# Two load queues, a pause in the zero fills, and three stage buffers in an attention and FFN backward kernel

## The chip, the cores and the metric

The kernel runs on one core of a Trainium2 chip. The metric is the device time of one execution in microseconds (us), the median of several runs. A profile gives the span of one execution, which is about 1.7 us below the time of that run (886.2 against 887.95 us before); positions in time below are read from the profiles, in us from the start of the span.

## The reference

It is one decode step (one query row) of an attention block and a gated FFN, with all gradients (shortened here):

```python
W = min(4096, max(256, Sk // 4))        # 4096 of the 32768 cached rows are attended
k = jnp.repeat(k_cache[:, :, Sk - W:, :], rep, axis=1)      # 8 groups, 2 heads each
v = jnp.repeat(v_cache[:, :, Sk - W:, :], rep, axis=1)
scores = jnp.einsum("bhqd,bhkd->bhqk", q, k) * (Dh ** -0.5)
o = jnp.einsum("bhqk,bhkd->bhqd", _softmax(scores, axis=-1), v)
# ...
h  = x + _A_ref(_layernorm(x), k_cache, v_cache, wq, wo)    # one query row, D = 448
h2 = h + _B_ref(_layernorm(h), w_gate, w_up, w_down)        # (g * u) @ w_down, F = 1792
# ...
_out, _vjp = jax.vjp(_f, x, k_cache, v_cache, wq, wo, w_gate, w_up, w_down)
return (_out, *_vjp(grad_out))          # the output and eight gradients
```

For time, one fact matters. The gradients of the two caches have 8 x 32768 x 256 elements each, but only the last 4096 rows of a group are attended. The other 28672 rows of each group must be written as zeros: 112 zero fills of 2 MB, 234.9 MB of the 332.75 MB that the kernel moves.

## The kernel before

The zero fills come from one zeroed tile in the core's memory (SBUF), 16 KB in each of 128 partitions. All but nine are sent by GpSimd, the nine others by SyncE, which also does every load and every other store:

```python
    LD = nc.sync
    ZQ = nc.gpsimd
    # ...
    late_jobs = [(out_2, G - 1, 5, 7, ZW), (out_3, G - 1, 0, 7, ZW)]
    for g in range(G):
        for o in (out_2, out_3):
            if g == G - 1 and o is out_3:
                continue
            reg = zero_rows(o, g, 0, 5 if g == G - 1 else NZ, ZW)
            for i in range(reg.shape[0]):
                ZQ.dma_start(out=reg[i], in_=zeros)
    # ... at the end of the program:
        for o, g, n0, n1, f in late_jobs:
            reg = zero_rows(o, g, n0, n1, f)
            for i in range(reg.shape[0]):
                LD.dma_start(out=reg[i], in_=zeros)
```

The work has three parts. *Attention* goes over eight groups; K and V of a group (2 MB each) are loaded into buffers that earlier groups free. The *FFN* goes over four blocks of weights in one buffer, so the loads of a block wait until the block before is computed; its gate and up rows are 1 KB long:

```python
    def load_ffn(f0, nw):
        n = 128 * nw
        LD.dma_start(out=wd_b[:, 0:nw, :], in_=B_w_down[f0:f0 + n, :].rearrange("(p w) n -> p w n", w=nw))
        for i, w in enumerate((B_w_gate, B_w_up)):
            LD.dma_start(out=w_b[i][:, 0:3 * n].rearrange("p (c f) -> p c f", c=3), in_=w[0:384, f0:f0 + n].rearrange("(p c) f -> p c f", c=3))
            LD.dma_start(out=wB_b[i][:, 0:n], in_=w[384:D, f0:f0 + n])
```

The *backward loop* follows, once more over the eight groups. Each group computes its gradients of V and K into two stage buffers of 2 MB and stores them; weight gradients are stored in between:

```python
    stage = [seq(MB), seq(MB + 16 * KB), seq(S[6])]
    # ...
            stV, stK = stage[stc % 2], stage[(stc + 1) % 2]
            if it >= 6:
                stV, stK = stage[(stc - 12) % 3], stage[(stc - 11) % 3]
            stc += 2
            # ... matmuls into PSUM, copied into stV and stK by VectorE and ScalarE
            for o_ap, st_ in ((out_3, stV), (out_2, stK)):
                LD.dma_start(out=o_ap[0, g, Sk - W:, :].rearrange("(p t) d -> p t d", t=T), in_=st_)
```

A scheduler orders the instructions of each engine; the program order is only a start. It moved the nine late fills of SyncE forward, among the K loads of attention.

Of the kernel before, what the change touches and what calls it, by code (L numbers as in the profile page):

```python
# [13 lines left out]
D = 448  # L14
H = 16
G = 8
Dh = 256
W = 4096
T = 32
# [4 lines left out]
Sk = 32768  # L24
EPS = 1e-5
SCALE = 1.0 / 16.0
ZW = 8192
NZ = (Sk - W) * Dh // (128 * ZW)
KB = 512


@with_exitstack
def kernel(
        ctx, tc, A_x, A_k_cache, A_v_cache, A_wq, A_wo, B_x, B_w_gate, B_w_up, B_w_down, grad_out,
           out_0, out_1, out_2, out_3, out_4, out_5, out_6, out_7, out_8):
    nc = tc.nc
    LD = nc.sync
    ZQ = nc.gpsimd

    const = ctx.enter_context(tc.tile_pool(name="const", bufs=1))  # L40
# [5 lines left out]

    MB = 128 * KB
    RB = 152 * KB
    TOTAL = 196 * KB
    arena = const.tile([128, TOTAL], bf16)  # L50

    def ar(off, n):
        return arena[:, off:off + n]

    def seq(off):
        return ar(off, T * Dh).rearrange("p (t d) -> p t d", d=Dh)

    zeros = ar(0, ZW)
    S = [16 * KB * (i + 1) for i in range(7)]
    V_at = [seq(o) for o in (S[5], S[0], S[1], S[2], S[3], S[4], S[6], S[5])]  # L60
    K_at = [seq(o) for o in (RB, S[6], S[4], S[5], RB, S[6], S[5], RB)]
    wqA = ar(S[2], 24 * KB).rearrange("p (c j) -> p c j", c=3)
    wqB = ar(S[2] + 24 * KB, 4 * KB)
    M_off = [MB + 4 * KB * g for g in range(6)] + [RB + 28 * KB, RB + 32 * KB]
# [6 lines left out]
    wo_sb = ar(RB, 28 * KB).rearrange("p (j n) -> p j n", n=D)  # L71
    wd_b = ar(RB + 28 * KB, 4 * D).rearrange("p (w n) -> p w n", n=D)
    w_b = [ar(RB + 63 * KB // 2 + 3 * KB * i, 3 * KB) for i in range(2)]
    wB_b = [ar(RB + 75 * KB // 2 + KB * i, KB)[0:64] for i in range(2)]
# [6 lines left out]
    ok_rows = ar(RB + 83 * KB // 2, 2 * KB)[0:H].bitcast(f32).rearrange("p (k d) -> p k d", k=2)  # L81
    h_row = ar(RB + 42 * KB, 2 * D)[0:1].bitcast(f32)

    stage = [seq(MB), seq(MB + 16 * KB), seq(S[6])]
    dq_bc = ar(RB + 8 * KB, H * Dh)
    Rbig = [ar(o, 8 * KB).rearrange("p (l n) -> p l n", l=8) for o in (RB + 16 * KB, S[1] + 24 * KB)]
    VT_slot = [ar(RB + (24 + 2 * i) * KB, 2 * KB).rearrange("p (e t k) -> p e t k", t=4, e=2) for i in range(3)]
# [10 lines left out]
    x_bf = const.tile([1, D], bf16)  # L98
    LD.dma_start(out=x_bf[:], in_=A_x.rearrange("a b d -> (a b) d"))
    dh2_bc = const.tile([128, D], bf16)  # L100
    LD.dma_start(out=dh2_bc[:], in_=grad_out.rearrange("a b d -> (a b) d").to_broadcast([128, D]))
    wq_A = A_wq[0:384, :].rearrange("(p c) j -> p c j", c=3)
    wq_B = A_wq[384:D, :].rearrange("r (h j) -> (r h) j", h=2)
    LD.dma_start(out=wqA, in_=wq_A)
    LD.dma_start(out=wqB, in_=wq_B)

    ident_bf = const.tile([128, 128], bf16)
    make_identity(nc, ident_bf[:])
# [11 lines left out]
    def zero_rows(o, g, n0, n1, f):  # L120
        reg = o[0, g, 0:Sk - W, :].rearrange("s d -> (s d)")[n0 * 128 * ZW:n1 * 128 * ZW]
        return reg.rearrange("(n p f) -> n p f", p=128, f=f)

    late_jobs = [(out_2, G - 1, 5, 7, ZW), (out_3, G - 1, 0, 7, ZW)]
    for g in range(G):
        for o in (out_2, out_3):
            if g == G - 1 and o is out_3:
                continue
            reg = zero_rows(o, g, 0, 5 if g == G - 1 else NZ, ZW)
            for i in range(reg.shape[0]):  # L130
                ZQ.dma_start(out=reg[i], in_=zeros)  # L131


    pair_f = const.tile([128, 64], f32)
# [68 lines left out]
        nc.vector.scalar_tensor_tensor(out=r[:], in0=t[:], scalar=rstd, in1=plus, op0=ALU.mult, op1=ALU.add)  # L203
        return r

    def load_kv(dst, cache, g):
        LD.dma_start(out=dst, in_=cache[0, g, Sk - W:, :].rearrange("(p t) d -> p t d", t=T))

    for g in range(3):
        load_kv(K_at[g], A_k_cache, g)  # L210
        load_kv(V_at[g], A_v_cache, g)

    rstd1, xnT_f, X1_b = layernorm(x_bf[:], bf16, "ln1")
    d2_ps = ps_t.tile([128, 4], f32, tag="tmp")
# [11 lines left out]
    qT_bf = const.tile([128, 32], bf16)  # L226
    nc.vector.tensor_copy(out=qT_bf[:], in_=qT_ps[:])

    load_kv(V_at[3], A_v_cache, 3)
    load_kv(V_at[4], A_v_cache, 4)  # L230

    def load_wo(j0, j1):
        LD.dma_start(out=wo_sb[:, j0:j1, :], in_=A_wo.rearrange("(p j) n -> p j n", j=32)[:, j0:j1, :])

    def load_ffn(f0, nw):
        n = 128 * nw
        LD.dma_start(out=wd_b[:, 0:nw, :], in_=B_w_down[f0:f0 + n, :].rearrange("(p w) n -> p w n", w=nw))
        for i, w in enumerate((B_w_gate, B_w_up)):
            LD.dma_start(out=w_b[i][:, 0:3 * n].rearrange("p (c f) -> p c f", c=3), in_=w[0:384, f0:f0 + n].rearrange("(p c) f -> p c f", c=3))
            LD.dma_start(out=wB_b[i][:, 0:n], in_=w[384:D, f0:f0 + n])  # L240

    pT_all = const.tile([128, G, T, 2], bf16)
    oT_f = const.tile([128, 2, H], f32)
# [32 lines left out]
    with tc.tile_pool(name="ps_x", bufs=1, space=bass.MemoryType.PSUM) as ps_x, \  # L276
# [69 lines left out]
        for g in range(G):  # L346
            p_f = p_next
            if g + 1 < G:
                p_next = scores(g + 1)
            moments(g, p_f)  # L350
            if g == 0:
                load_kv(K_at[3], A_k_cache, 3)
                load_kv(K_at[4], A_k_cache, 4)
            elif g == 1:
                load_kv(K_at[5], A_k_cache, 5)
            elif g == 2:
                load_kv(V_at[5], A_v_cache, 5)
            elif g == 3:
                load_kv(K_at[6], A_k_cache, 6)
                load_wo(19, 27)  # L360
            elif g == 4:
                load_kv(K_at[7], A_k_cache, 7)
            elif g == 5:
                load_kv(V_at[6], A_v_cache, 6)
            elif g == 6:
                load_kv(V_at[7], A_v_cache, 7)
                load_wo(27, 32)
        load_wo(0, 19)
        load_ffn(*FB[0])
        nc.vector.tensor_copy(out=ok_rows, in_=ok_ps[:])  # L370

    with tc.tile_pool(name="ps_mid", bufs=2, space=bass.MemoryType.PSUM) as ps_mid, \
# [27 lines left out]
        for q, (f0, nw) in enumerate(FB):  # L400
            n, cb = 128 * nw, f0 // 128
            if q:
                load_ffn(f0, nw)
            dh_f = workm.tile([128, 4], f32, tag="dh_f")
            for w in range(nw):
                nc.vector.tensor_tensor_reduce(out=dg_b[:, 0:D], in0=wd_b[:, w, :], in1=dh2_bc[:], scale=1.0, scalar=0.0,
                                               op0=ALU.mult, op1=ALU.add, accum_out=dh_f[:, w:w + 1])
            gu_ps = ps_mid.tile([128, 2, 4], f32, tag="mid")
            for i in range(2):
                wv = w_b[i][:, 0:3 * n].rearrange("p (c f) -> p c f", c=3)  # L410
                for w in range(nw):
                    for k in range(3):
                        nc.tensor.matmul(gu_ps[:, i, w:w + 1], lhsT=wv[:, k, w::nw], rhs=X2_b[:, k:k + 1], start=(k == 0), stop=False)  # L413
                    nc.tensor.matmul(gu_ps[:, i, w:w + 1], lhsT=wB_b[i][:, w:n:nw], rhs=X2_b[0:64, 5:6], start=False, stop=True)  # L414
            gu_f = workm.tile([128, 2, 4], f32, tag="gu_f")
            nc.vector.tensor_copy(out=gu_f[:, :, 0:nw], in_=gu_ps[:, :, 0:nw])  # L416
            for i in range(2):
                nc.vector.tensor_tensor(out=dgu_f[:, i, cb:cb + nw], in0=dh_f[:, 0:nw], in1=gu_f[:, 1 - i, 0:nw], op=ALU.mult)
            nc.vector.tensor_tensor(out=hh_f[:, cb:cb + nw], in0=gu_f[:, 0, 0:nw], in1=gu_f[:, 1, 0:nw], op=ALU.mult)
            nc.vector.tensor_copy(out=hh_bf[:, cb:cb + nw], in_=hh_f[:, cb:cb + nw])  # L420
            for i in range(2):
                spread(dg_b[:, i * KB:i * KB + n], diag_b, dgu_f[:, i, cb:cb + nw], nw, ps_mid, "mid")
            for w in range(nw):
                nc.tensor.matmul(ffn_ps[:], lhsT=hh_bf[:, cb + w:cb + w + 1], rhs=wd_b[:, w, :], start=(cb + w == 0), stop=(cb + w == NF - 1))
            for i in range(2):
                dg = dg_b[:, i * KB:i * KB + n]
                wv = w_b[i][:, 0:3 * n].rearrange("p (c f) -> p c f", c=3)
                for c in range(3):
                    nc.vector.tensor_tensor_reduce(out=wv[:, c, :], in0=wv[:, c, :], in1=dg, scale=1.0, scalar=0.0,
                                                   op0=ALU.mult, op1=ALU.add, accum_out=dhn2[:, c, 2 * q + i:2 * q + i + 1])  # L430
                nc.vector.tensor_tensor_reduce(out=wB_b[i][:, 0:n], in0=wB_b[i][:, 0:n], in1=dg[0:64, :], scale=1.0, scalar=0.0,
                                               op0=ALU.mult, op1=ALU.add, accum_out=dhnB[:, 2 * q + i:2 * q + i + 1])

        def close(dn, dcat):

# [58 lines left out]
    with tc.tile_pool(name="work2", bufs=2) as work2, tc.tile_pool(name="lnw", bufs=1) as lnw, \  # L494
# [82 lines left out]

        order = [1, 2, 3, 4, 5, 6, 7, 0]
        V_now = V_at[:]
        V_now[0] = seq(S[0])  # L580
        stc = 0
        for it, g in enumerate(order):
            V_sb = V_now[g]
# [5 lines left out]
                else:  # L589
                    nc.vector.tensor_copy(out=XT, in_=ps)  # L590
            dpT_ps = dots(V_sb, VT_slot, vpad[it % 2], rows2, ps_t, "tmp", evac)
            if it == 0:
                load_kv(V_now[0], A_v_cache, 0)
            if it == 4:
                LD.dma_start(out=wq2A, in_=wq_A)
# [20 lines left out]
            RB_ = Rbig[it % 2] if it >= 3 else Rbig[0]  # L616
            for l in range(8):
                nc.vector.tensor_scalar(out=RB_[:, l, :], in0=R_sb[:], scalar1=tl_f[:, l:l + 1], scalar2=None, op0=ALU.mult)
            stV, stK = stage[stc % 2], stage[(stc + 1) % 2]
            if it >= 6:  # L620
                stV, stK = stage[(stc - 12) % 3], stage[(stc - 11) % 3]
            stc += 2
            for l in range(8):
                for qp in range(2):
# [5 lines left out]
                    t = 4 * l + 2 * qp  # L630
# [27 lines left out]
                nc.vector.tensor_copy(out=dx_bf[:, 384:D], in_=dx_ps[0:1, 384:D])  # L658
                LD.dma_start(out=out_1.rearrange("a b d -> (a b) d"), in_=dx_bf[:])

        for o, g, n0, n1, f in late_jobs:
            reg = zero_rows(o, g, n0, n1, f)
            for i in range(reg.shape[0]):
                LD.dma_start(out=reg[i], in_=zeros)

# [1 line left out]
_INS = ['A_x', 'A_k_cache', 'A_v_cache', 'A_wq', 'A_wo', 'B_x', 'B_w_gate', 'B_w_up', 'B_w_down', 'grad_out']  # L667
# [26 lines left out]
```

## Time and profile before

| | before |
|---|---|
| median of 4 runs, on the chip that also ran the change | 887.32 us |
| bytes moved | 332.75 MB |
| attention ends (last output matmul of a group) | 365.0 us |
| output weights have landed | 410.8 us |
| backward loop starts (first query-gradient matmul) | 607.4 us |
| last copy into a stage buffer | 874.5 us |
| span | 886.2 us |

The profile cuts the span into 40 equal slices. A digit is the busy share of a slice in tenths; the last row is what the DMA engines moved. These are its rows for TensorE and DMA:

```profile
PE   0669999996059675504202020127986476644121
...
DMA  8999999999999999999999999999999198354444
GB/s 339 430 431 429 429 430 426 433 427 427 419 430 429 416 424 429 425 428 427 428 427 428 428 428 429 428 427 425 422 417 387 56 412 324 132 238 189 189 190 190
```

DMA is full (about 429 GB/s) up to the 31st slice, some 670 us, and then runs at 208 GB/s on average (680 to 875 us). TensorE, on the other hand, has long holes where DMA is full: the core waits for its own loads while the fills go through. The queues of the same page (packets, MB, and the time of their packets as a share of 16 engines) show who moves what; q0 is GpSimd's queue, q1 SyncE's:

```profile
q0 software_dynamic: 14832, 216.01, 57.5%
q1 hardware_dynamic: 13750, 116.19, 31.6%
...
HBM read 51.59 MB, written 280.59 MB: 375 GB/s over the span
```

The chain of waits follows the work that ended last backwards; each line is a start, a length and what was waited for. For a DMA the length runs from its issue to its landing. The engine that needs it may have worked for a part of that time, so a piece can be much longer than the engine's own wait. The longest DMA pieces after the start:

```profile
213.92 38.56 another core or an unknown queue
...
285.69 15.63 DMA arena<-in_A_v_cache_dram
...
326.34 16.25 DMA arena<-in_A_v_cache_dram
...
365.05 45.70 DMA arena<-in_A_wo_dram
...
434.35 40.05 DMA arena<-in_B_w_up_dram
...
485.24 39.58 DMA arena<-in_B_w_up_dram
...
534.79 37.56 DMA arena<-in_B_w_up_dram
...
668.90 28.69 DMA out_dram<-arena
...
803.71 10.57 DMA out_dram<-arena
...
828.96 10.57 DMA out_dram<-arena
```

The piece at 213.92 is a wait for K. Its load sits in SyncE's queue behind the nine fills that the scheduler had moved forward. Then come V loads of two groups, the output weights, and 37 to 40 us for each of three FFN blocks. In the backward loop a store of weight gradients takes 28.69 us. The two pieces of 10.57 us are stage stores that a stage copy waits for.

Why an FFN load of 1.3 MB takes 40 us is shown by the packets of the two queues from 375 to 395 us, when the first block is loaded:

```profile
q0 software_dynamic: 554, 8.04, 93.9%
q1 hardware_dynamic: 553, 0.53, 7.6%
```

The two queues take turns, one packet each: 554 against 553. But a packet of a fill has 16 KB and one of the load 1 KB or less, so the load gets 0.53 of 8.58 MB, 27 GB/s.

### The profile page before, as it was taken

The numbers are of one execution on the slowest core, as the hardware profiler recorded it, in microseconds if no ns is written. First come the engines' busy times: TensorE is split into PE (matmuls) and PEld (weight loads), VectorE is DVE, ScalarE is ACT, GpSimd is POOL, SyncE is SP. The second block draws the span as 40 slices with busy tenths as digits, with TensorE's granted clock in tenths as the row PEclk, the third lists the DMA queues.
The fourth block names the chain that finished last, engine by engine and source line by source line (L and its number), as shares of the span: only waits on it lengthen the run. The fifth ranks groups of instructions, "written<-read, shape, count | busy, mean of one in ns | idle before, by whom it ended". The sixth has DMA issues, their size and how long they took to land.

```text
span 886.2 us, 8621 instructions
## 1 busy us (share of the span) xinstructions
PE 458.8 (52%) x3193; PEld 248.1 (28%) x3193; DVE 370.8 (42%) x1243; ACT 198.7 (22%) x325; POOL 59.7 (7%) x112
## 2 busy tenths in 40 slices
PE   0669999996059675504202020127986476644121
PEld 0435455453025242302100000016643233221000
DVE  2036535633015244200403111083396779986453
ACT  0341331330031300000000000001462443433342
POOL 4000000000001000000000010010000000000000
PEclk9969999999579897856555555556997687666555
DMA  8999999999999999999999999999999198354444
GB/s 339 430 431 429 429 430 426 433 427 427 419 430 429 416 424 429 425 428 427 428 427 428 428 428 429 428 427 425 422 417 387 56 412 324 132 238 189 189 190 190
DMA packets 28624, 332.75 MB, mean 375 GB/s; under 512 B 2979, under 2 KB 7206, under 8 KB 8742
## 3 DMA queue, kind: packets, MB, share of 16 engines
q0 software_dynamic: 14832, 216.01, 57.5%
q1 hardware_dynamic: 13750, 116.19, 31.6%
q8 instruction: 25, 0.41, 0.2%
q14 instruction: 17, 0.14, 0.0%
HBM read 51.59 MB, written 280.59 MB: 375 GB/s over the span
## 4 chain that ended last, share of the span: by engine, by line
PE 38%; DMA 34%; DVE 16%; another core or an unknown queue 4%; ACT 4%; issue 1%; SPq 1%; DVEq 0%; ACTq 0%
DMA arena<-in_B_w_up_dram 13%; PE M_ps L327 12%; PE ok_ps L331 6%; DMA out_dram<-arena 6%; PE rows_ps L267 6%; DMA arena<-in_A_k_cache_dram 5%; DMA arena<-in_A_wo_dram 5%; PE tr_ps L264 4%; DMA arena<-in_A_v_cache_dram 4%; DVE arena L636 3%; DVE arena L635 3%; PE d_ps L628 2%; DVE arena L458 2%; ACT arena L282 2%; PE dqb_ps L501 2%
## 5 line engine op out<-in xcount | busy, mean ns | idle before, releaser
L323 DVE TENSOR_SCALAR arena<-arena,p_f 128x256 bf16<-128x256 bf16 x512 | 109.4, 281 | 132.0 <-PE M_ps L327 132.0
L327 PE MATMUL M_ps<-arena 128*128 128x512 bf16 x512 | 124.9, 387 | 22.3 <-DMA arena<-in_A_v_cache_dram 22.3
L264 PE MATMUL tr_ps<-ident_bf,arena 128*128 128x128 bf16 x1024 | 88.2, 237 | 75.2 <-DMA arena<-in_A_k_cache_dram 49.7
L264 PEld LDWEIGHTS <-arena 128*128 128x128 bf16 x1024 | 67.3, 106 | 119.6 <-DMA arena<-in_A_k_cache_dram 50.2
L267 PE MATMUL rows_ps<-arena,vpad 128*16 128x512 bf16 x256 | 84.4, 429 | 31.0 <-DVE arena L590 15.0
L282 ACT COPY arena<-tr_ps 128x1024 bf16<-128x1024 bf16 x64 | 61.8, 1015 | 145.3 <-PE tr_ps L264 145.3
L131 POOL DMA_DIRECT2D out_dram<-arena x103 | 55.1, 536 | 576.6 <-DMA out_dram<-arena 576.6
L628 PE MATMUL d_ps<-arena,rT 32*128 32x512 bf16 x256 | 39.9, 518 | 71.9 <-DVE arena L636 46.1
L327 PEld LDWEIGHTS <-arena 128*128 128x128 bf16 x512 | 47.0, 100 | 75.6 <-DMA arena<-in_A_v_cache_dram 22.7
L413 PE MATMUL gu_ps<-X_b,arena 128*128 128x1 bf16 x84 | 7.2, 177 | 111.5 <-DMA arena<-in_B_w_gate_dram 70.4
L331 PE MATMUL ok_ps<-arena 128*16 128x256 bf16 x512 | 57.5, 273 | 0.9 <-DVE arena L309 0.9
L635 DVE CAST arena<-d_ps 128x512 bf16<-128x512 f32 x64 | 44.0, 687 | 29.4 <-PE d_ps L628 22.0
L632 ACT CAST arena<-d_ps 128x512 bf16<-128x512 f32 x64 | 37.8, 590 | 73.7 <-PE d_ps L628 52.0
L331 PEld LDWEIGHTS <-arena 128*16 128x16 bf16 x512 | 45.4, 90 | 13.9 <-issue 3.4
L636 DVE CAST arena<-d_ps 128x512 bf16<-128x512 f32 x64 | 43.6, 681 | 12.9 <-DMA out_dram<-arena 12.9
L188 ACT CAST arena<-bc_ps 128x256 bf16<-128x256 f32 (+1 forms) x32 | 11.1, 347 | 156.3 <-PE bc_ps L187 155.1
L588 ACT COPY arena<-tr_ps 128x1024 bf16<-128x1024 bf16 x32 | 32.7, 1021 | 49.4 <-PE tr_ps L264 25.7
L416 DVE COPY gu_f<-gu_ps 128x8 f32<-128x8 f32 (+1 forms) x4 | 0.7, 166 | 102.9 <-PE gu_ps L414 102.9
L633 ACT CAST arena<-d_ps 128x512 bf16<-128x512 f32 x64 | 38.2, 597 | 21.3 <-DMA out_dram<-arena 21.3
L628 PEld LDWEIGHTS <-rT 32*128 32x128 bf16 x256 | 10.0, 96 | 97.0 <-DVE arena L636 57.1
L267 PEld LDWEIGHTS <-vpad 128*16 128x16 bf16 x256 | 19.5, 91 | 62.3 <-issue 44.7
L413 PEld LDWEIGHTS <-arena 128*128 128x128 bf16 x84 | 5.0, 119 | 112.9 <-DMA arena<-in_B_w_gate_dram 71.3
(192 smaller groups left out, 405.6 us busy)
## 6 DMA issues: line engine op xcount, KB each, us to landing
out_dram<-arena POOLq DMA_DIRECT2D x103, 2048.0 KB, 45.6
out_dram<-arena SPq DMA_DIRECT2D x25, 2048.0 KB, 10.7
arena<-in_A_v_cache_dram SPq DMA_DIRECT2D x9, 2048.0 KB, 52.3
arena<-in_A_k_cache_dram SPq DMA_DIRECT2D x8, 2048.0 KB, 47.8
arena<-in_A_wq_dram SPq DMA_DIRECT2D x2, 3072.0 KB, 14.6
out_dram<-arena SPq DMA_DIRECT2D x3, 1344.0 KB, 15.2
out_dram<-arena SPq DMA_DIRECT2D x3, 1024.0 KB, 11.8
out_dram<-arena SPq DMA_DIRECT2D x2, 1456.0 KB, 12.9
```

Of the source, the lines that this page charges most:

```text
L131: ZQ.dma_start(out=reg[i], in_=zeros)
L264: nc.tensor.transpose(tr_ps[:, dh, i, :], X_sb[:, 4 * q + i, dh * 128:(dh + 1) * 128], ident_bf[:])
L267: nc.tensor.matmul(rows_ps[:], lhsT=pad[:, dh, 16 * q:16 * q + 16], rhs=XT[:, dh].rearrange("p t k -> p (t k)"), start=(q == 0 and dh == 0 ...
L282: sT_ps = dots(K_at[g], KT_slot, vpad[g % 2], rows1, ps_c, "cols", lambda q, XT, ps: nc.scalar.copy(out=XT, in_=ps))
L323: nc.vector.tensor_scalar(out=pK[:, i, hh, :], in0=K_sb[:, t, :], scalar1=p_f[:, 8 * i + c, hh:hh + 1], scalar2=None, op0=ALU.mult)
L327: nc.tensor.matmul(M_ps[vh][:], lhsT=V_sb[:, t, vh * 128:(vh + 1) * 128], rhs=pK[:, i, :, :].rearrange("p h d -> p (h d)"), start=(t == 0) ...
L331: nc.tensor.matmul(ok_ps[:, k, :], lhsT=ppad[g % 2][:, 8 * (t % 4) + t // 4, :], rhs=X_sb[:, t, :], start=(g == 0 and k == 0 and t == 0), ...
L628: nc.tensor.matmul(d_ps[:, qi].rearrange("p w d -> p (w d)"), lhsT=rT[32 * q:32 * (q + 1), :], rhs=RB_[32 * q:32 * (q + 1), l, :], start=T ...
L632: nc.scalar.copy(out=stV[:, t:t + 2, :], in_=d_ps[:, :, 0, :])
L633: nc.scalar.copy(out=stK[:, t:t + 2, :], in_=d_ps[:, :, 1, :])
L635: nc.vector.tensor_copy(out=stV[:, t:t + 2, :], in_=d_ps[:, :, 0, :])
L636: nc.vector.tensor_copy(out=stK[:, t:t + 2, :], in_=d_ps[:, :, 1, :])
```

## The change

The intent is to take the loads out of the fills' way where compute waits for them, and to send the fills where the DMA engines have room. K and V loads, and a small part of the query weights, are divided over SyncE and ScalarE (`LV`). GpSimd sends 50 fills, then waits for the last FFN load, then sends 38. SyncE sends three fills after the last V load and three behind each FFN block, and nine at the very end, now held in program order. The backward loop rotates over three stage buffers; V of group 0 is reloaded later to make room.

```diff
+NPRE = 50
+NLATE = 9
+    LV = nc.scalar
-    stage = [seq(MB), seq(MB + 16 * KB), seq(S[6])]
+    stage = [seq(MB), seq(MB + 16 * KB), seq(S[0])]
     # ...
+    fills = [zero_rows(o, g, 0, NZ, ZW)[i] for g in range(G) for o in (out_2, out_3) for i in range(NZ)]
+    def fill(eng, n):
+        last = None
+        for _ in range(n):
+            last = tc.keep_in_program_order(eng.dma_start(out=fills.pop(0), in_=zeros))
+        return last
+    fill(ZQ, NPRE)
     # ...
     for g in range(3):
-        load_kv(K_at[g], A_k_cache, g)
-        load_kv(V_at[g], A_v_cache, g)
+        load_kv(K_at[g], A_k_cache, g, LV if g == 0 else LD)
+        load_kv(V_at[g], A_v_cache, g, LD if g == 0 else LV)
     # ... (V of groups 3 to 6 through LV too; loads in program order)
                 load_wo(27, 32)
+                fill(LD, 3)
         load_wo(0, 19)
         load_ffn(*FB[0])
+        fill(LD, 3)
     # ...
             if q:
                 load_ffn(f0, nw)
+                fill(LD, 3)
     # ... after the FFN:
+        rest = fills[:-NLATE]
+        for i, f in enumerate(rest):
+            ins = ZQ.dma_start(out=f, in_=zeros)
+            if i == 0:
+                tc.add_manual_dep(ins..., ffn_last..., reason="loads first")
     # ... backward loop:
-        V_now[0] = seq(S[0])
+        V_now[0] = seq(S[6])
-            if it == 0:
+            if it == 5:
                 load_kv(V_now[0], A_v_cache, 0)
-            stV, stK = stage[stc % 2], stage[(stc + 1) % 2]
-            if it >= 6:
-                stV, stK = stage[(stc - 12) % 3], stage[(stc - 11) % 3]
+            stV, stK = stage[stc % 3], stage[(stc + 1) % 3]
     # ...
+        for f in fills[-NLATE:]:
+            tc.keep_in_program_order(LD.dma_start(out=f, in_=zeros))
```

One thing is not in the diff. The fills after the pause are not held in program order, and the built program has the one with the wait in tenth place: GpSimd sends 59 fills before it pauses, and 29 after.

More of the change, by code (lines that the diff above doesn't have):

```diff
@@ L104 @@
     LD.dma_start(out=wqA, in_=wq_A)
-    LD.dma_start(out=wqB, in_=wq_B)
+    LV.dma_start(out=wqB, in_=wq_B)
     ident_bf = const.tile([128, 128], bf16)
@@ L122, in zero_rows @@
         return reg.rearrange("(n p f) -> n p f", p=128, f=f)
-    late_jobs = [(out_2, G - 1, 5, 7, ZW), (out_3, G - 1, 0, 7, ZW)]
-    for g in range(G):
-        for o in (out_2, out_3):
-            if g == G - 1 and o is out_3:
-                continue
-            reg = zero_rows(o, g, 0, 5 if g == G - 1 else NZ, ZW)
-            for i in range(reg.shape[0]):
-                ZQ.dma_start(out=reg[i], in_=zeros)
+    fills = [zero_rows(o, g, 0, NZ, ZW)[i] for g in range(G) for o in (out_2, out_3) for i in range(NZ)]
[5 more added lines that the diff above has]
+    fill(ZQ, NPRE)
     pair_f = const.tile([128, 64], f32)
@@ L204, in layernorm_bwd, with load_kv @@
         return r
-    def load_kv(dst, cache, g):
-        LD.dma_start(out=dst, in_=cache[0, g, Sk - W:, :].rearrange("(p t) d -> p t d", t=T))
+    def load_kv(dst, cache, g, eng=None):
+        tc.keep_in_program_order((eng or LD).dma_start(out=dst, in_=cache[0, g, Sk - W:, :].rearrange("(p t) d -> p t d", t=T)))
     for g in range(3):
-        load_kv(K_at[g], A_k_cache, g)
-        load_kv(V_at[g], A_v_cache, g)
+        load_kv(K_at[g], A_k_cache, g, LV if g == 0 else LD)
+        load_kv(V_at[g], A_v_cache, g, LD if g == 0 else LV)
     rstd1, xnT_f, X1_b = layernorm(x_bf[:], bf16, "ln1")
@@ L227 @@
     nc.vector.tensor_copy(out=qT_bf[:], in_=qT_ps[:])
-    load_kv(V_at[3], A_v_cache, 3)
-    load_kv(V_at[4], A_v_cache, 4)
+    load_kv(V_at[3], A_v_cache, 3, LV)
+    load_kv(V_at[4], A_v_cache, 4, LV)
     def load_wo(j0, j1):
-        LD.dma_start(out=wo_sb[:, j0:j1, :], in_=A_wo.rearrange("(p j) n -> p j n", j=32)[:, j0:j1, :])
+        tc.keep_in_program_order(LD.dma_start(out=wo_sb[:, j0:j1, :], in_=A_wo.rearrange("(p j) n -> p j n", j=32)[:, j0:j1, :]))
+    ffn_last = [None]
     def load_ffn(f0, nw):
         n = 128 * nw
-        LD.dma_start(out=wd_b[:, 0:nw, :], in_=B_w_down[f0:f0 + n, :].rearrange("(p w) n -> p w n", w=nw))
+        tc.keep_in_program_order(LD.dma_start(out=wd_b[:, 0:nw, :], in_=B_w_down[f0:f0 + n, :].rearrange("(p w) n -> p w n", w=nw)))
         for i, w in enumerate((B_w_gate, B_w_up)):
-            LD.dma_start(out=w_b[i][:, 0:3 * n].rearrange("p (c f) -> p c f", c=3), in_=w[0:384, f0:f0 + n].rearrange("(p c) f -> p c f", c=3))
-            LD.dma_start(out=wB_b[i][:, 0:n], in_=w[384:D, f0:f0 + n])
+            tc.keep_in_program_order(LD.dma_start(out=w_b[i][:, 0:3 * n].rearrange("p (c f) -> p c f", c=3), in_=w[0:384, f0:f0 + n].rearrange("(p c) f -> p c f", c=3)))
+            ffn_last[0] = tc.keep_in_program_order(LD.dma_start(out=wB_b[i][:, 0:n], in_=w[384:D, f0:f0 + n]))
     pT_all = const.tile([128, G, T, 2], bf16)
@@ L356 @@
             elif g == 2:
-                load_kv(V_at[5], A_v_cache, 5)
+                load_kv(V_at[5], A_v_cache, 5, LV)
             elif g == 3:
@@ L363 @@
             elif g == 5:
-                load_kv(V_at[6], A_v_cache, 6)
+                load_kv(V_at[6], A_v_cache, 6, LV)
             elif g == 6:
@@ L432 @@
                                                op0=ALU.mult, op1=ALU.add, accum_out=dhnB[:, 2 * q + i:2 * q + i + 1])
+        rest = fills[:-NLATE]
+        for i, f in enumerate(rest):
+            ins = ZQ.dma_start(out=f, in_=zeros)
+            if i == 0:
+                tc.add_manual_dep(ins.ins if hasattr(ins, "ins") else ins, ffn_last[0].ins.name, mybir.DependencyInfo(mybir.DependencyClass.Sync, mybir.DependencyReason.DATA), reason="loads first")
         def close(dn, dcat):
@@ L659 @@
                 LD.dma_start(out=out_1.rearrange("a b d -> (a b) d"), in_=dx_bf[:])
-        for o, g, n0, n1, f in late_jobs:
-            reg = zero_rows(o, g, n0, n1, f)
-            for i in range(reg.shape[0]):
-                LD.dma_start(out=reg[i], in_=zeros)
+        for f in fills[-NLATE:]:
+            tc.keep_in_program_order(LD.dma_start(out=f, in_=zeros))
 _INS = ['A_x', 'A_k_cache', 'A_v_cache', 'A_wq', 'A_wo', 'B_x', 'B_w_gate', 'B_w_up', 'B_w_down', 'grad_out']
```

## The prediction

> **What bounds it now.** The DMA row of the 40 slices is saturated (425 to 431 GB/s) until about 670 us, then runs at 190 to 240 GB/s to the end at 886. The queues table has 332.75 MB; at 429 GB/s that alone is 776 us. So DMA is full for three quarters and half idle for the last. Meanwhile the chain of waits shows compute starved by its own loads: 38.6 us at 213.9 (a K load behind nine fills that the scheduler had hoisted into SyncE's queue), V loads 15.6 and 16.3, output weights 45.7, and FFN blocks at 40.1, 39.6 and 37.6 us.
>
> Why the FFN loads are slow: two queues with 16 KB packets get about 215 GB/s each, but FFN rows of 1 KB get about 27 GB/s beside fills at 400. The Trainium skill, "DMA: Bandwidth & Descriptors", section "Queues, rings and completion order", says that each DMA engine round-robins between queues by packet; this trace agrees. A third queue changes shares, not the sum.
>
> **The change.** No bytes and no arithmetic go; 112 fills remain. 50 are sent early by GpSimd, 15 by SyncE (three after the last V load, three behind each FFN block), 38 by GpSimd afterwards, 9 by SyncE last. In the built instruction order the wait for the last FFN load sits on the tenth of the 38, not the first, so 59 run before the pause. The V0 reload moves late, and the backward stores rotate over three stage buffers.
>
> **Estimate, from those durations.**
> - Attention start: K1 stays near 50 us (its queue has 7.3 MB ahead at a third of 430). The 38.6 us wait goes; the two V waits stay. Attention ends near 326 instead of 365.
> - By then GpSimd has sent some 94 of its 124 MB. Output weights, behind three SyncE fills, land near 345 (was 411).
> - FFN block 0 still meets fills: some 40 us, to about 385. Block 1 comes behind three fills and the rest of GpSimd's: near 425. GpSimd pauses: blocks 2 and 3 come about 20 us apart (6.3 MB of fills, 14.6 us, then 1.3 MB), landing near 465 (was 572).
> - Before, 35 us pass from there to the query-gradient matmuls (607.5): now about 498, 109 us earlier.
> - Backward was 267 us to its last staged copy. The remaining 29 GpSimd fills now share DMA with its stores until about 690; the third buffer should give back the loss and 5 us more. Last copy near 762.
> - Then two stores and nine fills: 23 MB, 54 us.
>
> 109 + 5 us go, 54 less the old tail's 11 come back. **Predicted 816 us**, 8 in 10 between 790 and 838. Floor about 784. Chances: faster 0.96, same 0.03, slower 0.01.
>
> **What would show it.** DMA row near 430 until the last few slices; no 38 us K wait; FFN waits of about 40, 40, 20, 20 us; query-gradient matmuls near 500; stage copies waiting for stores more often between 560 and 690; a last stretch of about 45 us of fills alone, engines idle.
>
> **What would make it wrong.** If fewer early fills remain at the FFN, its blocks go faster and the time falls towards 785. If stores under the resumed fills stall the backward loop by 10 us or more per group, or small loads run slowly even alone, it passes 830. If loads through ScalarE's queue block its copies, attention lengthens.

## The result and the profile after

The change takes 838.56 us (837.28 to 839.29, 4 runs) against 887.32 us. A ratio here is the mean time of one kernel's runs over that of the other's in the same rounds, so not quite the ratio of the medians: 0.9448, 95% interval 0.9431 to 0.9464. It is 5.5% faster. The predicted 816 us with 790 to 838 had promised a gain of 71 us; the gain was 49 us, and the time lies 0.6 us above the range.

| position, us | before | predicted | after |
|---|---|---|---|
| attention ends | 365.0 | 326 | 332.4 |
| output weights landed | 410.8 | 345 | 354.9 |
| FFN block 0 complete | | 385 | 396 |
| backward loop starts | 607.4 | 498 | 503.2 |
| last stage copy | 874.5 | 762 | 780.2 |
| length of the loop | 267.1 | 264 | 277.0 |
| last copy to the end | 11.7 | 54 | 56.1 |
| span | 886.2 | 816 | 836.3 |

The same rows of slices:

```profile
PE   0739999999994929041122319984534466542000
...
DMA  9999999999999999999999999999999987644699
GB/s 347 430 431 428 430 428 429 425 428 423 422 428 421 429 416 428 424 429 427 429 418 403 397 428 419 421 420 423 422 425 407 424 343 332 277 201 201 288 426 389
```

DMA is now full until some 680 us of 836 instead of 670 of 886, falls to 200 GB/s, and is full again in the last slices while all engines stand still. The queues, with ScalarE's as q10:

```profile
q0 software_dynamic: 12672, 184.56, 52.3%
q1 hardware_dynamic: 14758, 132.44, 38.1%
q10 hardware_dynamic: 1152, 15.20, 4.3%
```

The chain of waits after the change, from the V loads on:

```profile
247.15 15.68 DMA arena<-in_A_v_cache_dram
...
292.62 15.91 DMA arena<-in_A_v_cache_dram
...
335.39 42.85 DMA arena<-in_B_w_gate_dram
379.44 13.41 another core or an unknown queue
...
402.70 28.73 DMA arena<-in_B_w_gate_dram
...
439.75 10.05 DMA arena<-in_B_w_gate_dram
...
457.52 9.71 DMA arena<-in_B_w_gate_dram
...
565.95 30.07 DMA out_dram<-arena
...
606.69 28.73 DMA out_dram<-arena
...
642.47 41.27 DMA out_dram<-arena
```

The wait for K at 214 us is gone. The two V waits (15.68 and 15.91 us) are as before. The FFN blocks wait 42.85 and 13.41, 28.73, 10.05 and 9.71 us: the first two still meet fills of GpSimd. In the backward loop there are now three pieces of 30.07, 28.73 and 41.27 us for stores, where before there was one of 28.69 and two of 10.57. All three are stores of weight gradients, and each ends at a write of VectorE (line 533) into one of the two weight-gradient buffers, not at a stage copy. How long the engines themselves waited for DMA in the loop is told by the view of waits (engine, line, what it waited for; us in total, times, longest). Lines 647 and 650 are stage copies, line 658 uses the reloaded query weights:

```profile
ACT arena L647 <- DMA out_dram<-arena: 48.7, 7, 13.5
...
DVE arena L650 <- DMA out_dram<-arena: 21.4, 4, 8.8
DVE arena L533 <- DMA out_dram<-arena: 18.4, 5, 5.8
...
DVE arena L658 <- DMA arena<-in_A_wq_dram: 6.5, 1, 6.5
```

VectorE thus waits 46.3 us in the loop, 21.4 of them for stage buffers. Before, it was 22.6 us: 20.2 for stage buffers, 2.4 for a weight-gradient buffer.

The view of windows gives, for a stretch, the busy time of each engine, the granted clock, the DMA share and the GB/s (last column):

```profile
562.00:680.00 118.00, 57.64 (x399) 27.75 (x398) 72.01 (x166) 38.63 (x61) 3.76 (x7) 0.68 1.01 420
680.00:780.00 100.00, 45.47 (x293) 17.73 (x293) 75.34 (x140) 45.27 (x80) 0.00 (x0) 0.62 0.57 237
780.00:836.00 56.00, 0.00 (x0) 0.00 (x0) 0.20 (x1) 0.03 (x1) 0.00 (x0) 0.50 0.97 412
```

From 680 to 780 us DMA moves 237 of 429 GB/s, so 45 us of its time are unused, and directly after come 56 us of stores and fills with nothing else going on.

### The profile page after: what moved, and what is told of

It reads as the page before. It is cut to its first block, busy times and chain, and to the rows that moved or that the text cites. A ratio compares the mean times of both kernels' runs of the same rounds, so it can differ in the third digit from the quotient of the medians.

```text
span 836.3 us, 8603 instructions
## 1 busy us (share of the span) xinstructions
PE 461.8 (55%) x3193; PEld 248.7 (30%) x3193; DVE 371.5 (44%) x1243; ACT 198.5 (24%) x325; POOL 51.9 (6%) x97
## 3 DMA queue, kind: packets, MB, share of 16 engines
HBM read 51.59 MB, written 280.59 MB: 397 GB/s over the span
## 4 chain that ended last, share of the span: by engine, by line
PE 39%; DMA 31%; DVE 13%; ACT 4%; another core or an unknown queue 4%; issue 1%; SPq 0%; DVEq 0%; ACTq 0%
DMA out_dram<-arena 13%; PE M_ps L334 13%; DMA arena<-in_B_w_gate_dram 11%; PE ok_ps L338 7%; PE rows_ps L274 7%; PE tr_ps L271 4%; DMA arena<-in_A_v_cache_dram 4%; DMA arena<-in_A_wq_dram 3%; DVE arena L649 3%; ACT arena L289 3%; DVE arena L650 2%; DVE arena L474 2%; PE d_ps L642 2%; PE dqb_ps L517 2%
## 5 line engine op out<-in xcount | busy, mean ns | idle before, releaser
L271 PE MATMUL tr_ps<-ident_bf,arena 128*128 128x128 bf16 x1024 | 90.5, 238 | 55.1 <-DMA arena<-in_A_k_cache_dram 31.0
L274 PE MATMUL rows_ps<-arena,vpad 128*16 128x512 bf16 x256 | 87.1, 438 | 30.2 <-DVE arena L606 22.0
L271 PEld LDWEIGHTS <-arena 128*128 128x128 bf16 x1024 | 67.7, 106 | 102.1 <-issue 50.9
L334 PEld LDWEIGHTS <-arena 128*128 128x128 bf16 x512 | 46.9, 100 | 81.1 <-DMA arena<-in_A_v_cache_dram 28.0
L650 DVE CAST arena<-d_ps 128x512 bf16<-128x512 f32 x64 | 43.5, 680 | 21.5 <-DMA out_dram<-arena 21.4
L132 POOL DMA_DIRECT2D out_dram<-arena x50 | 27.1, 543 | 274.6 <-DMA out_dram<-arena 274.6
L604 ACT COPY arena<-tr_ps 128x1024 bf16<-128x1024 bf16 x32 | 32.7, 1021 | 42.2 <-DVE doX_f L474 23.5
L274 PEld LDWEIGHTS <-vpad 128*16 128x16 bf16 x256 | 19.1, 91 | 64.2 <-issue 50.6
L446 POOL DMA_DIRECT2D out_dram<-arena x38 | 20.2, 532 | 282.4 <-DMA out_dram<-arena 188.8
L416 DVE CUSTOM_DVE_ANT_0 arena<-arena,dh_bc 128x448 bf16<-128x448 bf16 x14 | 8.8, 625 | 61.2 <-DMA arena<-in_B_w_down_dram 60.8
## 6 DMA issues: line engine op xcount, KB each, us to landing
out_dram<-arena SPq DMA_DIRECT2D x3, 1344.0 KB, 22.1
```

The source lines that it names most:

```text
L271: nc.tensor.transpose(tr_ps[:, dh, i, :], X_sb[:, 4 * q + i, dh * 128:(dh + 1) * 128], ident_bf[:])
L274: nc.tensor.matmul(rows_ps[:], lhsT=pad[:, dh, 16 * q:16 * q + 16], rhs=XT[:, dh].rearrange("p t k -> p (t k)"), start=(q == 0 and dh == 0 ...
L334: nc.tensor.matmul(M_ps[vh][:], lhsT=V_sb[:, t, vh * 128:(vh + 1) * 128], rhs=pK[:, i, :, :].rearrange("p h d -> p (h d)"), start=(t == 0) ...
L604: nc.scalar.copy(out=XT, in_=ps)
L650: nc.vector.tensor_copy(out=stK[:, t:t + 2, :], in_=d_ps[:, :, 1, :])
```

## The experiments

The question: the loop was to shrink a little and grew by 10 us. My theory was that the 29 resumed fills cost the loop far more than I had assumed. Rivals: SyncE's own crowded queue, or the third buffer being of no use. (My expectations below, e1's and b4's above all, take the lengths of chain pieces for waits of an engine, and those of the loop for waits of stage copies; the view of waits above corrects that.) Further runs ask what each part of the change is worth, and why a fill costs what it does. Each was run beside the kernel before on the same chip, whose median was 888.26 us for the first eight, 887.44 for the next three and 887.06 for the last. "Loop" is always from the first query-gradient matmul to the last stage copy. All results were correct.

### e1: the resumed fills moved to the tail

```diff
-NLATE = 9
+NLATE = 38
```

> All but one of the 29 zero fills that GpSimd sends after the pause go to SyncE's tail, so the backward stores have the DMA engines to themselves; nothing else changes. Theory (the backward loop lost its time to the resumed fills): the query-gradient matmuls still start near 503 us, the last staged copy comes 245 to 255 us after them instead of 277, and no stage copy waits over 15 us for a store (30, 29 and 41 us in the changed kernel). The tail of 38 fills then takes 38 x 4.9 = 186 us, total near 950 us. Rival (SyncE's own queue, with weight gradients, the query weights and V0 between the stores, is what makes stage copies wait): the loop stays at 270 us or more, waits near 30 to 40 us stay, total 970 or more.

Measured: 930.22 us (2 runs). The loop starts at 498.3 and takes **231.4 us** instead of 277.0, even less than the theory said. These two are all that is left in the loop's chain of DMA pieces over 5.5 us:

```profile
688.49 6.30 DMA out_dram<-arena
...
708.82 6.29 DMA out_dram<-arena
```

VectorE's waits for DMA in the loop fall from 46.3 to 4.4 us; none is left for the weight-gradient buffers. So the resumed fills cost the loop 45.6 us, and SyncE's own queue alone is not the cause: it holds the same stores and loads here. (One fill is still sent after the pause; it ends before the first store.)

### e2: the old stage buffers

```diff
-    stage = [seq(MB), seq(MB + 16 * KB), seq(S[0])]
+    stage = [seq(MB), seq(MB + 16 * KB), seq(S[6])]
-        V_now[0] = seq(S[6])
+        V_now[0] = seq(S[0])
-            if it == 5:
+            if it == 0:
-            stV, stK = stage[stc % 3], stage[(stc + 1) % 3]
+            stV, stK = stage[stc % 2], stage[(stc + 1) % 2]
+            if it >= 6:
+                stV, stK = stage[(stc - 12) % 3], stage[(stc - 11) % 3]
```

> The changed kernel with the stage buffers, the place of V0 and the time of its reload as before the change. Theory (the third buffer did give time back, and the fills took more than that): the loop from the query-gradient matmuls to the last staged copy grows from 277 to 290 to 300 us, total 851 to 861 us. Rival (the third buffer is worth nothing while stores run at half rate, or the late V0 reload costs what it gives): the loop stays within 5 us of 277 and the total within 5 us of 838.6.

Measured: 860.18 us (4 runs), ratio to before 0.9696 (0.9672 to 0.972). The loop takes 299.1 us. The new rotation with its place and time for V0 is worth 22.1 us under the fills. It does give time back: VectorE waits 42.8 us for stage buffers in this run and 21.4 in the changed kernel. Its waits for the weight-gradient buffers stay (17.5 and 18.4 us). Against the kernel before, which has the same buffers and rotation, the loop of this run is 32.0 us longer (299.1 against 267.1): that is what the resumed fills add to the old loop, which had met fills itself (GpSimd's queue moves 50.6 MB in this loop and 23.5 in that one). The run undoes three edits at once, so it doesn't say which of them earns.

### e3: the pause where it was meant

```diff
-            ins = ZQ.dma_start(out=f, in_=zeros)
+            ins = tc.keep_in_program_order(ZQ.dma_start(out=f, in_=zeros))
```

> The fills of GpSimd after the pause are kept in program order, so that the pause begins after 50 fills, not 59. Theory: FFN block 0 waits under 20 us for its loads and block 1 near 15 (42 and 29 in the changed kernel), the query-gradient matmuls start near 460 instead of 503; but 38 fills instead of 29 then meet the backward stores, so the loop grows from 277 to about 300 and the total falls to only 815 to 828 us. Rival (the resumed fills do not slow the loop): the loop stays at 277 and all of the 43 us is gained, total near 795.

Measured: 831.74 us (4 runs), ratio 0.9375 (0.9351 to 0.9399). The loop starts at 459.7 as expected, 43.5 us earlier, and takes 313.5 us, 36.5 us longer. Lines of its chain:

```profile
332.30 37.22 DMA arena<-in_B_w_gate_dram
...
377.83 10.07 DMA arena<-in_B_w_gate_dram
...
522.17 30.03 DMA out_dram<-arena
...
562.89 28.44 DMA out_dram<-arena
...
598.39 47.55 DMA out_dram<-arena
646.57 21.63 DMA out_dram<-arena
...
669.61 39.03 DMA out_dram<-arena
```

The wait of block 0 fell only to 37.22 us, not under 20, because fills sent before the pause were still going through: GpSimd's queue moved 264 GB/s from 340 to 360 us, and its last packet ended at 368.8 us, just before the wait did (369.5). Blocks 1 to 3 wait some 10 us each. In the loop the chain now has five long pieces for stores instead of three; loop and total are both above what I expected. Of 43.5 us gained ahead of the loop, 7 remain: the fills that left the FFN stand in the loop.

### e4: the nine late fills between the stores

```diff
             for o_ap, st_ in ((out_3, stV), (out_2, stK)):
                 LD.dma_start(out=o_ap[0, g, Sk - W:, :]..., in_=st_)
+            if it >= 3:
+                for _ in range(2):
+                    if late:
+                        tc.keep_in_program_order(LD.dma_start(out=late.pop(0), in_=zeros))
```

> The nine fills of SyncE's tail are sent two by two behind the stage stores of the fourth group on. Theory (the DMA engines are half idle from 680 to 780 us in the changed kernel, and the tail of 45 us is work that fits in there): total 795 to 805 us, the last store almost at the end. Rival (fills in front of stores make the stage copies wait as the fills of GpSimd do): the loop grows by 30 us or more, and the total stays over 825 us.

Measured: **808.57 us** (4 runs), ratio 0.9115 (0.9086 to 0.9144), a little above the expected range. The loop grows by only 6.7 us to 283.7, and the tail is almost gone: the last copy is at 787.0 and the span 806.4. The same nine fills cost about 45 us at the end and about 15 here. Behind the stores in *their own* queue these fills used idle time. But they differ from GpSimd's fills in two things, the queue and the time: the first of them is sent at 693.9 us, when GpSimd's fills have ended (682 us) and DMA is half idle. Which of the two counts, this run does not show.

### e5: no pause

```diff
-            if i == 0:
+            if False:
                 tc.add_manual_dep(...)
```

> The changed kernel without the wait of GpSimd's fills for the last FFN load; the fills of SyncE between the blocks stay. Theory (the pause earns the FFN time: with 16 KB fills on another queue a block's rows of 1 KB come at 27 GB/s): blocks 1 to 3 take some 65 us each (three fills at half rate, 29 us, then 40 us of load), the query-gradient matmuls start at 600 to 640 us instead of 503, the loop then runs free of fills in about 231 us, total 890 to 925 us. Rival (the sum of bytes decides and the pause only moves waits): total within 10 us of 838.6.

Measured: 931.88 us (2 runs), worse than the kernel before, and a little above the expected range. The loads of block 1 take 45 and then 13 us, and block 2 likewise; each also stands behind SyncE's own fills:

```profile
407.98 45.08 DMA arena<-in_B_w_gate_dram
454.25 13.44 another core or an unknown queue
```

The loop starts at 643.2 us, and, free of fills, takes 230.4 us: a second reading of what e1 showed. The pause is thus the part that carries the change: taking it away costs 93 us, more than the whole gain. Without it the blocks come some 70 us apart (last landings at 400.5, 470.7, 540.9 and 608.1 us); in the kernel before, without SyncE's fills between the blocks, the last two landed 50.4 and 47.5 us after the block in front of them.

### e6: one load queue

```diff
-    LV = nc.scalar
+    LV = nc.sync
```

> The changed kernel with all K and V loads on SyncE's queue, none on ScalarE's. Theory (a second load queue changes shares and adds no bandwidth; attention is bound by TensorE and by when buffers come free): attention ends within 6 us of the 332 us of the changed kernel, total 832 to 845 us. Rival (the second queue is what shortened attention): attention ends at 345 us or later, total 850 or more.

Measured: 834.99 us (4 runs), ratio 0.9414 (0.9386 to 0.9442). Attention ends at 326.9 us, 5.5 us *earlier* than with two queues. (The edit moves the small part of the query weights to SyncE as well.) Single profiles scatter: the eight runs with two queues and the same 16 KB fills end attention between 330.6 and 337.4 us. Both runs with one queue and the late fills out of the way, this one and e7, lie below that (326.9 and 325.7), so the direction holds; the size is uncertain by some us.

The Trainium skill, "DMA: Bandwidth & Descriptors", section "Issuing engines are not separate DMA queues", says that issuing from several engines "will only save the time on the sequencer it takes to initiate the DMA". This run agrees: the second load queue earned nothing. Why it costs 5.5 us of attention I only infer: with three queues taking turns, each of the first loads has a third of the rate, and by the chain of waits the transposes of the second group begin at 54.8 us in the changed kernel and at 52.4 in this run. The later part isn't a clean comparison, since the scheduler put the pause after 56 fills here, not 59.

### e7: the kernel before with only its late fills kept late

```diff
             for i in range(reg.shape[0]):
-                LD.dma_start(out=reg[i], in_=zeros)
+                tc.keep_in_program_order(LD.dma_start(out=reg[i], in_=zeros))
```

> The kernel before with one edit: the nine fills of SyncE's queue are kept in program order, so that they come last instead of among the K loads. Theory (the 38.6 us wait for K in attention came from these fills): attention ends near 326 us instead of 365, the query-gradient matmuls start near 569 instead of 607, and 44 us of fills stand at the end instead of 11 us of stores; some of GpSimd's fills end earlier, total 860 to 870 us. Rival (K was late for another reason): attention still ends near 365 and the total rises above 900.

Measured: 887.37 us (4 runs), ratio 1.0004 (0.997 to 1.0039): the same. The first lines of its chain that are DMA, after the start:

```profile
245.70 14.94 DMA arena<-in_A_v_cache_dram
...
286.85 15.21 DMA arena<-in_A_v_cache_dram
...
325.73 45.83 DMA arena<-in_A_wo_dram
```

The wait for K is gone and attention ends at 325.7 us, so the nine fills were its cause. The loop starts 40 us earlier and ends 47 us earlier (827.2). Nearly all of it is given back, because the fills that had caused the wait now stand alone at the end: 55.9 us from the last copy to the end, 11.7 before. I had expected 860 to 870 us, since I thought the loop would be shorter by more than it was (259.8 us against 267.1).

### e8: the kernel before with fills in pieces of 4 KB

```diff
+    zsmall = zeros[:, 0:2048].unsqueeze(1).to_broadcast([128, 4, 2048])
+    def zq(dst):
+        return ZQ.dma_start(out=dst.rearrange("p (a f) -> p a f", a=4), in_=zsmall)
-                ZQ.dma_start(out=reg[i], in_=zeros)
+                zq(reg[i])
```

> The kernel before, with GpSimd's 103 fills cut into pieces of 4 KB (a source of 4 KB per partition, read four times) instead of 16 KB; same bytes, same queues, same order. Theory (each DMA engine takes a packet from one queue and a packet from the next, so the fills' share goes with their packet size): rows of 1 KB get about 1/5 of 430 GB/s instead of 27, an FFN block's load waits 13 to 18 us instead of 38 to 40, loads and stores of 16 KB packets get 4/5, and the fills yield to everything and end last; query-gradient matmuls near 455 to 480 us, total 785 to 815 us. Rival (the two queues share by time or bytes whatever the packets' size, or 4 KB pieces are themselves slow): FFN waits stay at 35 us or more, total within 10 us of 888 or above.

Measured: **822.57 us** (4 runs), ratio 0.9262 (0.9242 to 0.9282): this one edit to the kernel before beats the whole change. The packets of the two queues from 20 to 40 us:

```profile
q1 hardware_dynamic: 458, 6.70, 78.3%
q0 software_dynamic: 460, 1.82, 22.2%
```

Again one for one, 460 against 458, but now the loads have the large packets and move 6.70 of 8.54 MB, where they had about half with fills of 16 KB. The theory's direction holds throughout. The last load of an FFN block takes 12.2 to 14.9 us from issue to landing (13 to 18 expected, 37.6 to 40.4 before), the loop starts at 444.2 us, earlier than expected, DMA is full to the end, and the fills end last, 87.0 us after the last copy. The total is above the expected 785 to 815 us. Pieces of 4 KB are not free, as windows with no DMA but fills show (e8 first, then the kernel before):

```profile
770.00:800.00 30.00, 0.00 (x0) 0.00 (x0) 0.00 (x0) 0.00 (x0) 1.40 (x2) 0.50 1.02 403
```

```profile
590.00:620.00 30.00, 16.89 (x85) 13.75 (x86) 15.93 (x63) 2.80 (x4) 3.19 (x6) 0.64 1.01 426
```

403 against 426 GB/s. (The source differs too, 4 KB read four times, so that the size of the pieces is the only reason is not shown.) And the fills now meet every group of the loop, which takes 289.8 us with its two stage buffers.

### e9 and b2: small pieces in the changed kernel

e9 is the changed kernel with GpSimd's fills through the same `zq`; b2 adds the edit of e4.

> The changed kernel with GpSimd's 88 fills in pieces of 4 KB; SyncE's 24 fills stay at 16 KB. Theory (the resumed fills cost the backward loop because their 16 KB packets take every second turn): FFN block 0 waits 15 to 20 us instead of 43, query-gradient matmuls at 455 to 475 us, and the loop falls from 277 to 240 to 258 us although more than 29 fills meet it; total 785 to 805 us. Rival (fills cost the loop by the bytes they move): the loop stays at 277 us or grows, total 820 or more.

> The changed kernel with GpSimd's fills in pieces of 4 KB and the nine late fills between the stage stores, both as in the single trials. Theory: near the floor of bytes (332.75 MB at 429 GB/s is 776 us, and some 8 us of start): total 784 to 797 us. Rival (the two edits give the same gain, not the sum): within 3 us of the better of the two alone, 805 or more.

Measured: e9 814.8 us (ratio 0.9176, 0.9159 to 0.9193), b2 814.8 us (0.9189, 0.9158 to 0.9221), 4 runs each. Both missed their ranges. In e9 the loop falls to 262.5 us, although fills of GpSimd go on to the end of it (40.8 MB of them after the first store, against 27.2 MB in the changed kernel): with small packets more fills cost the loop less. That speaks against a cost by bytes alone. FFN blocks wait 21 to 23 us each, the last two longer than in the changed kernel (10 us), and the loop starts at 482.4, later than expected. SyncE's own fills of 16 KB still stand ahead of the loads. And GpSimd hardly pauses: its small fills go so slowly that it waits only 11.8 us for the last FFN load, where 94.2 us lie between its 59th and 60th fill in the changed kernel, so its fills run beside all four blocks. b2 gains nothing on e9 and is slower than e4 alone (808.57 us, and the intervals of the ratios do not meet), so its theory and its rival both missed. In e9 DMA is already full, at 394 to 430 GB/s in all of the 40 slices but the first and the last, so there is hardly any idle time left to fill.

### b1 and b4: fills by group

b1 has the pause after 50 fills (e3), 21 fills of GpSimd after it, and three fills of SyncE behind every group's stores. b4 moves them away from groups 3 and 4.

```diff
-NLATE = 9
+NLATE = 26
             # behind the two stores of a group:
+            for _ in range(3):                              # b1
+            for _ in range((3, 3, 3, 1, 1, 4, 4, 0)[it]):   # b4
+                if late:
+                    tc.keep_in_program_order(LD.dma_start(out=late.pop(0), in_=zeros))
```

> The pause after 50 fills, only 21 fills of GpSimd after it (about what the DMA engines can move until the first backward store), and 24 of the remaining 26 fills on SyncE's queue, three behind the stage stores of each of the eight groups. Theory (fills cost the loop when a second queue takes half the rate from its stores; behind the stores in the same queue they fill idle time): query-gradient matmuls near 460 us, loop 290 to 320 us with the DMA row near 425 GB/s throughout, total 792 to 806 us, better than the 808.6 of the variant with nine fills between stores. Rival (any fill in the loop costs its own 4.9 us): loop 340 us or more, total 815 or more.

> The variant with three fills behind every group's stores, with the fills moved away from groups 3 and 4: 3, 3, 3, 1, 1, 4, 4, 0 behind the eight groups and seven at the end. Reason: in that variant VectorE stood 36.5 us at 633 us for the reload of the query weights, which had queued behind stores and fills. Theory (fills in the stores' own queue cost only where a load that compute needs soon comes behind them): that wait falls under 20 us, the loop from 300 to 270 to 285 us, total 795 to 803 us. Rival (the loop is bound by bytes whatever the places of the fills): the loop gives back what the tail takes, total 804 to 810 us.

Measured: b1 **805.8 us** (ratio 0.9082, 0.9055 to 0.9108), b4 **805.4 us** (0.9079, 0.9061 to 0.9098), 4 runs each; with e4 they are the fastest of all and beat both kernels. b1's chain has this piece:

```profile
633.04 36.51 DMA arena<-in_A_wq_dram
```

It is the load of the query weights, which had queued behind stores and fills, from issue to landing; VectorE itself waited only 5.4 us at its end. In b4 that piece is 26.51 us (VectorE's wait 2.6) and the loop 285.7 instead of 300.3 us, but the total is the same: the seven fills at the end take what the loop gave. b1's total is at the upper end of its expected range. b4 missed all three of its numbers, and its total is what the rival said. Both move 332.75 MB in a span of about 804 us, 414 GB/s on average, against 429 GB/s when DMA is full; some 28 us of DMA time remain unused, at the start, in the FFN, and in the loop.

## Why the prediction was wrong

- *Right: what bounds the kernel.* The K wait went (none of 38 us; e7 shows its cause). The FFN waits came as 43 and 13, 29, 10 and 10 us (predicted 40, 40, 20, 20), so blocks 2 and 3 passed undisturbed, and blocks 0 and 1 met the fills that the built order had let through. The loop started at 503.2 us, predicted 498. Between attention's end and the loop's start lie 170.8 us, predicted 172; single terms of that sum are off by up to 5 us in both directions, so that it fits so closely is partly luck.
- *Right: the tail.* 56.1 us from the last copy to the end, predicted 54.
- *Wrong, the step that failed:* "The remaining 29 GpSimd fills now share DMA with its stores until about 690; the third buffer should give back the loss and 5 us more. Last copy near 762." The sharing ended at 682 us, as said. But the fills add 32.0 us to the old loop (e2 against before), and the new buffers give back 22.1 (e2 against after): 267.1 + 32.0 - 22.1 = 277.0 us, not 264. That is 13 of the 20 us that the span is off. I had never put a number on the loss, nor seen that the old loop of 267 us, my base, was itself no measure of a loop free of fills (that took 231.4 us with the new buffers, e1; against that the fills cost 45.6 us, 46.6 by e5).
- *The path that it had wrong:* only a part of the loss is waiting for stage buffers. Of the 41.9 us that VectorE waits more than in e1, 17.0 are for stage buffers; 18.4 are for the two weight-gradient buffers, which the third stage buffer did nothing for (17.5 in e2), and 6.5 for the query weights. The chain's three longest pieces in the loop end at the weight-gradient buffers. This is read from the view of waits; no run had a third weight-gradient buffer, so what it would be worth stays open.
- *Mis-sized, smaller:* attention ended 6 us late. "A third queue changes shares, not the sum" was right, but the change in shares was a loss: with one load queue attention ends at 326.9 (e6), the predicted 326. The tail and the stretch before the loop together add about 1 us, and the time outside the span 1.7 us.
- *The risk was named* ("stores under the resumed fills stall the backward loop by 10 us or more per group"), but the third buffer was trusted to cover it. One of its signs did not come: "DMA row near 430 until the last few slices"; from 680 to 780 us DMA ran at 237 GB/s.

How the cost arises is shown by the packet counts, e8 and e9: queues take turns by packet, so a fill of 16 KB packets takes half of the rate from stores of the same packet size, and stage and weight-gradient buffers are free later. Sent in the stores' own queue, and after the fills of the other queue had ended, nine fills cost the kernel a third of what they cost alone at the end (e4). What remains open is how the 22 us of e2 divide among its three edits, and whether the queue or the time makes e4's fills cheap.

## What to carry to other kernels

Where DMA is full for most of a kernel, look for the time in which it is *not* full, and move the transfers that nobody waits for there; removing a wait only pays if the transfer that caused it doesn't stand alone somewhere else afterwards (e7 gained 47 us up to the last copy and lost 44 behind it). Bulk transfers in another queue take turns by packet with the loads and stores that compute needs: pause them, cut their pieces smaller, or send them behind the urgent ones when DMA has room. Before crediting a buffer with hiding a new contention, take the contended loop's cost as a number of its own, check whether the old loop was contended already, and look which buffers the engines wait for, in the view of waits as well as in the chain: here more than half of VectorE's added waiting was for buffers that the change did not touch.

## What the Trainium skill lacked or had wrong

- "DMA: Bandwidth & Descriptors", section "Queues, rings and completion order", has the round robin by packet, and the runs agree (554 packets against 553, 460 against 458). What it lacks is the consequence: a queue's share goes with its packet size. Rows of 1 KB got 27 of 429 GB/s beside pieces of 16 KB, and cutting the pieces to 4 KB took the kernel before from 887 to 823 us.
- The same page, section "Specifications", gives 512 B or more as the size of a transfer for line rate. Fills in pieces of 4 KB ran at 403 GB/s, of 16 KB at 426. By that row both should be at line rate; the difference is small, and the 4 KB source was read four times, which may have a part in it.
- The same section gives an HBM limit of about 358 GB/s for a core, a stack's 716 GB/s divided by two cores. That is a share, and the row alone can be misread as a bound for a kernel on one core: this core moved about 429 GB/s over most of its span, and 280.59 of the 332.75 MB were writes to HBM.
- The same page, section "Issuing engines are not separate DMA queues", says what a second issuing engine does not bring, which e6 confirms; it doesn't say that it can hurt. With K and V on two queues, attention ended 5.5 us later than in e6 (3.7 to 10.5 us over the eight profiles with two queues).
